# Turned exponentials read back from HBM in one transfer a tile in place of four, and the last x of a U projection split one slot sooner

## The chip, the core and the metric

The kernel runs on one core of one Trainium2 chip. The metric is device time in microseconds (us) of one execution, lower is better. The core has four engines that matter here: TensorE (PE: matmuls, and PEld: the loading of their stationary operand), VectorE (DVE), ScalarE (ACT) and GpSimd (POOL). SyncE (SP) issues most DMA transfers, ScalarE some. 16 DMA engines move the data between HBM and the on-chip memory of 128 partitions.

## What is computed

Chunked attention, then a low-rank mixer, then a two-layer network. The inputs are q, k and v of (8 batches, 8 heads, 576 positions, 64), U (576 x 32), V (32 x 576), w_ch1 (512 x 2048) and w_ch2 (2048 x 512), all float32 or wider:

```python
scores = scale * q_c @ k_c^T              # within chunks of 64 positions, per batch and head
attn = exp(scores - max(scores)); attn = attn / (sum(attn) + 1e-9)
x = attn @ v_c                            # heads side by side: (8, 576, 512)
u = x + ((x^T @ U) @ V)^T                 # mixes positions, rank 32
out = u + relu(u @ w_ch1) @ w_ch2
```

## The kernel before

**Tiles and pairs.** Two batches form a pair (four pairs, 0 to 3), and a pair has nine tiles of 128 positions (t = 0 to 8). Three tiles form a group for the two-layer network. A block is one group with one of the 16 slices of w_ch1 and w_ch2: `hidden` (line 748) makes h with 12 matmuls, ScalarE and VectorE take relu apart into a high and a low part (`relu_high`, `relu_low`, lines 756 and 761), and `project_out` (line 774) adds three times three matmuls into the output banks. So every value is carried as a high and a low float32r part, and each product is made of three.

**Two ways of ordering.** The lead (weights, tiles of pair 0, and the first blocks) is ordered by a planner with costs. From there the order is written out by hand: the loop at line 980 goes through the blocks, and each block has four slots, `j` = 0 to 3. At each slot it first runs what the dictionary `agenda` holds for that slot, in the order in which `at` put it there, and then the output products of the block before (`flush`). Slots are numbered through: `FIRST` is 128, a pair has `PAIR` = 192. Every engine does its instructions in this order, each waiting only for its own data and for the room that it writes.

**Attention of pairs 1 to 3.** ScalarE issues `permute` transfers (line 580), 288 KB each, which copy q and k in HBM into blocks of 32 (`qblocks`, `kblocks`). A `Tile` then does its steps at slots relative to its own slot s (`plan_tile`, line 901): `load` of q and k at s - 9, `turn` at s - 4 (VectorE transposes in blocks of 32), `load_v` at s + 1, `turn_ex` and `sums` at s + 2, `put_ex` at s + 3, `get_ex` at s + 6. At s itself runs `both` (line 945): the value products of the tile before (`values`, line 675), the scores of this one (line 622), its softmax up to the exponential (lines 635, 636, 642), and then `scaled` of the tile before (line 687), which makes its x. The chain of these slots is written out at line 932: tiles of pair 1 from t = 2 follow each other after 10, 10, 10, 12 and 20 slots, those with t = 7 and 8 after 11 and more.

**The turned exponentials.** The value products need the exponentials with keys on partitions. VectorE transposes within blocks of 32 (`exb`, line 653), and the blocks are moved across partitions through HBM. `put_ex` (line 657) stores 32 partitions of `exb` in each of four transfers, 512 bytes a piece, into a room of [g 4, k 32, a 4, (h i) 128]. `get_ex` (line 664) reads it back in four transfers, one for each a, to 128 partitions (g k), in pieces of 32 numbers (128 bytes) that go to `eT[:, h, a, :]`. Each of the eight is 64 KB. All are issued by SP, whose instructions wait in order: for the data, and for a semaphore to be free, of which the transfers of SP and ScalarE share eight in turn.

**U projections.** A pair has two (e = 0, 1), each over five x (`project_ops`, line 487): `high` copies x to `xh` (ScalarE, line 496), `low` makes `xl` = x - `xh` (VectorE, line 500), `product` is two matmuls on `ust` (lines 507 and 508), and the last step also evacuates y (lines 517 and 518). `plan_proj` (line 921) puts `high` of the i-th x at a slot s, `low` at s + 1 and `product` at s + 4. The five start at made - 3 to made + 1, where made is the slot at which `both` makes the last x.

**Mixes.** `plan_mix` (line 913): `low_rank` (line 535) and `add` (line 541) at s, `turn` at s + 1, `put` (line 718) of four transfers `xs<-xb` at s + 2, `get` (line 724), one transfer `uf<-xs` of 256 KB, at s + 5, and `split` (lines 737 and 738) at s + 10, which makes `uth` and `utl` for `hidden`. The first three mixes of a pair are planned from made + 8 of its fifth x on, two slots apart; the next three from made + 8 of its last.

**V in the lead.** Three transfers bring V to 128 partitions (`v_ops`, line 244): the load at line 252 and the store at line 261 with `"r (b c) -> b r c"`, b = 4, and the spread at line 265, which reads rows four times over:

```python
nc.sync.dma_start(st["all"], st["rows"].unsqueeze(0).broadcast_to([4, R, S]))
```

Most tiles that live for a short time (raw, turned and split q, k, v, `ex`, `exb`, `eT`, `xh`, `xl`, `xb`, `uf`) share one set of eight buffers of 2 KB a partition (`slot`, line 74).

## Time and profile before

| what | us |
|---|---|
| median of 3 runs | 977.58 (976.29 to 980.03) |
| the profiled execution, its own time | 977.97 |
| its span, first to last instruction | 976.2 |
| TensorE busy in the span | 927.3 (95%) |
| VectorE busy | 457.6 (47%) |
| ScalarE busy | 234.7 (24%) |
| mean granted TensorE clock | 0.982 |

A row of the profile has the engine, the line of the kernel, what is written from what, and times in us from the start of the span. PE rows overlap, since matmuls are pipelined: two rows that begin 0.24 us apart and last 0.40 us are a TensorE at work without a gap. A bracket at the end of a row tells how long the engine was idle before it and what it waited for. Rows of SPq and ACTq are instructions that issue transfers; their length is the time to issue, and the time to landing is told apart. The first 92 us are the lead, with the first attention tiles and weights; from some 236 us on the tiles go through `put_ex` and `get_ex`.

### The profile page before, as it was taken

Reading aid. Unit: us, or ns where it says so; the run is one execution under the profiler, and the core shown is the slowest. Engines: PE = TensorE matmul, PEld = TensorE weight load, DVE = VectorE, ACT = ScalarE, POOL = GpSimd, SP = SyncE. Lnnn points to the kernel's source line nnn. Section 1 sums busy time; section 2 is a strip of 40 time slices with the busy share of each in tenths; the row PEclk is TensorE's granted clock in tenths of the full one; section 3 lists DMA queues with packets and bytes.
Section 4 is the critical chain, followed back from the end, with each engine's and each line's share of the span. In section 5 each row is a group of like instructions: output and inputs, shape, how many; then the busy total and the mean of one; then the engine's idle time right before and its main releaser. Section 6 shows DMA issues by size and latency. Waiting matters only on the chain.

```text
span 976.2 us, 16189 instructions
## 1 busy us (share of the span) xinstructions
PE 927.3 (95%) x6624; PEld 819.7 (84%) x6624; DVE 457.6 (47%) x898; ACT 234.7 (24%) x413; POOL 23.7 (2%) x53
## 2 busy tenths in 40 slices
PE   5477999999999999999999999999999999999998
PEld 4355888998888888888889888898889988999997
DVE  3398998223465555543641455543551443321211
ACT  4465565111121122111221122111211122111110
POOL 7200000000000000000000000000000000000000
PEclk9778999999999999999999999999999999999999
DMA  9963237455768635542483635453241312110000
GB/s 187 200 200 114 100 132 165 65 116 129 130 124 179 139 76 122 126 113 55 105 180 56 146 67 120 110 118 77 65 117 25 90 31 65 57 42 1 33 1 33
DMA packets 298631, 97.84 MB, mean 100 GB/s; under 512 B 230140, under 2 KB 287740, under 8 KB 298556
## 3 DMA queue, kind: packets, MB, share of 16 engines
q1 hardware_dynamic: 186044, 80.28, 33.2%
q10 hardware_dynamic: 111360, 14.16, 9.2%
q0 software_dynamic: 1152, 2.36, 1.2%
q8 instruction: 52, 0.85, 0.4%
q14 instruction: 23, 0.19, 0.1%
HBM read 73.61 MB, written 37.30 MB: 114 GB/s over the span
## 4 chain that ended last, share of the span: by engine, by line
PE 85%; DVE 4%; SPq 4%; DMA 3%; issue 2%; ACT 2%; ACTq 0%; DVEq 0%
PE h L748 40%; PE o L774 38%; PE as L675 2%; PE as L622 1%; PE u L535 1%; SPq L360 1%; SPq L361 1%; DMA qblocks<-in_q_dram 1%; DMA wraw<-in_moe_w_ch_dram 1%; PE y L508 1%; SPq L297 1%; DMA eT<-exs 1%; PE y L507 1%; DVE x L786 1%; ACT hh L756 0%
## 5 line engine op out<-in xcount | busy, mean ns | idle before, releaser
L748 PE MATMUL h<-uth,w 128*128 128x384 f32 x1536 | 425.1, 339 | 3.1 <-ACT uth L737 1.4
L774 PE MATMUL o<-w,hh 128*128 128x512 f32 x1152 | 364.5, 398 | 0.0
L761 DVE SCALAR_TENSOR_TENSOR hl<-h,hh 128x384 fp32r<-128x384 f32 x192 | 106.7, 556 | 423.6 <-ACT hh L756 423.0
L748 PEld LDWEIGHTS h<-uth,w 128*128 128x128 f32 x1536 | 282.0, 188 | 12.2 <-ACT uth L737 1.9
L748 PE MATMUL h<-utl,w 128*128 128x384 f32 x768 | 260.3, 339 | 0.8 <-DVE utl L738 0.4
L774 PEld LDWEIGHTS o<-w,hh 128*128 128x128 f32 x1152 | 212.4, 188 | 36.2
L756 ACT ACTIVATE hh<-h 128x384 fp32r<-128x384 f32 x192 | 94.4, 492 | 564.2 <-PE h L748 556.5
L774 PE MATMUL o<-w,hl 128*128 128x512 f32 x576 | 227.4, 395 | 0.0
L748 PEld LDWEIGHTS h<-utl,w 128*128 128x128 f32 x768 | 144.6, 188 | 9.2 <-DVE utl L738 0.7
L774 PEld LDWEIGHTS o<-w,hl 128*128 128x128 f32 x576 | 108.4, 188 | 25.8 <-DVE hl L761 0.3
L786 DVE TENSOR_TENSOR x<-o,x 128x512 f32<-128x512 f32 x48 | 31.5, 682 | 4.8 <-PE o L774 4.7
L642 ACT ACTIVATE ex<-ex 128x512 f32<-128x512 f32 x25 | 15.8, 632 | 68.2 <-DVE ex L636 68.2
L500 DVE TENSOR_TENSOR xl<-x,xh 128x512 fp32r<-128x512 f32 x40 | 26.3, 678 | 8.8 <-ACT xh L496 8.8
L496 ACT CAST xh<-x 128x512 fp32r<-128x512 f32 x40 | 24.2, 616 | 19.6 <-DVE x L454 5.6
L635 DVE TENSOR_REDUCE mx<-as 128x4 f32<-128x256 f32 x50 | 20.9, 418 | 12.9 <-PE as L622 11.4
L541 DVE TENSOR_TENSOR x<-u,x 128x512 f32<-128x512 f32 x36 | 23.9, 677 | 4.7 <-PE u L535 4.7
L675 PEld LDWEIGHTS as<-vn,eT 64*64 64x64 f32 x800 | 15.1, 134 | 11.4 <-issue 10.4
L370 POOL DMA_DIRECT2D qkv<-in_v_dram x36 | 22.3, 635 | 4.2 <-DMA qkv<-in_v_dram 3.1
L738 DVE TENSOR_TENSOR utl<-uf,uth 128x512 fp32r<-128x512 f32 x27 | 18.4, 684 | 8.4 <-ACT uth L737 8.2
L508 PE MATMUL y<-xl,ust 128*128 128x512 f32 x40 | 17.1, 428 | 5.2 <-DVE xl L500 5.2
L636 DVE TENSOR_TENSOR ex<-as,mx 128x256 f32<-128x256 f32 x50 | 21.2, 424 | 1.7
L675 PE MATMUL as<-vn,eT 64*64 64x64 f32 x800 | 19.0, 224 | 2.9 <-DMA eT<-exs 2.3
(85 smaller groups left out, 531.8 us busy)
## 6 DMA issues: line engine op xcount, KB each, us to landing
wraw<-in_moe_w_ch_dram SPq DMA_DIRECT2D x32, 512.0 KB, 3.7
out_dram<-x SPq DMA_DIRECT2D x36, 256.0 KB, 2.0
vn<-in_v_dram SPq DMA_DIRECT2D x108, 64.0 KB, 2.6
qblocks<-in_q_dram ACTq DMA_DIRECT2D x24, 288.0 KB, 3.9
kblocks<-in_k_dram ACTq DMA_DIRECT2D x24, 288.0 KB, 4.1
xs<-xb SPq DMA_DIRECT2D x108, 64.0 KB, 1.8
uf<-xs SPq DMA_DIRECT2D x27, 256.0 KB, 2.9
exs<-exb SPq DMA_DIRECT2D x100, 64.0 KB, 1.8
```

What stands on the lines that cost most here:

```text
L370: (nc.gpsimd if early(pr, t) else nc.sync).dma_start(vn[e * C : (e + 1) * C, c, :, 0:D], v[b, e::2, s0 : s0 + C, :].rearrange("h s d -> s ...
L496: nc.scalar.copy(st["h"], x_of[pr, i + 4 * e])
L500: nc.vector.tensor_sub(st["l"], x_of[pr, i + 4 * e], st["h"])
L508: nc.tensor.matmul(ps, lhsT=lhs, rhs=st["l"], start=False, stop=(i == 4))
L541: nc.vector.tensor_add(x, st["u"], x)
L636: nc.vector.tensor_sub(self.ex[:, e].rearrange("p b h k -> p h b k"), self.sc[e].rearrange("p (h b k) -> p h b k", b=2, k=TB), mx[:, e].un ...
L675: nc.tensor.matmul(ps[e][cs, (HP + hp) * C : (HP + hp + 1) * C], lhsT=self.eT[rows, hp, 2 * c : 2 * c + 2, :].rearrange("p a i -> p (a i)" ...
L748: nc.tensor.matmul(ps[:, :GN], lhsT=w[:, z, cc], rhs=u[:, cc, :], start=(n == 0), stop=(n == 3 * NCC - 1))
L756: nc.scalar.activation(hh, ps[:, :GN], AF.Relu)
L761: nc.vector.scalar_tensor_tensor(hl, ps[:, :GN], 0.0, hh, op0=ALU.max, op1=ALU.subtract)
L774: nc.tensor.matmul(acc[j], lhsT=h[:, js], rhs=w2[f][:, z], start=(first and i == 0), stop=(final and i == 2),)
L786: nc.vector.tensor_add(x, ps, x)
```

## The change

Three edits. The room of the turned exponentials is laid out as [k 32, (g h) 16, a 4, i 32], so that what one partition (g k) of `eT` needs lies in one run of 2 KB; `get_ex` becomes one transfer, and the four of `put_ex` now write pieces of 32 numbers (128 bytes) where they wrote 128 numbers. The fifth x of a U projection has its `high`, `low` and `product` one slot sooner (`high` at made, `low` at made + 1, `product` and the evacuation of y at made + 4). The first six mixes of a pair are planned one slot sooner as a whole.

```diff
         def put_ex(self):
-            self.room = dram.tile([NQ, TB, NQ, HP * TB], F32, name="exs_" + self.n)
+            self.room = dram.tile([TB, NQ * HP, NQ, TB], F32, name="exs_" + self.n)
             for a in range(NQ):
                 nc.sync.dma_start(
-                    self.room[:, :, a].rearrange("g k x -> k g x"), self.exb[a * TB : (a + 1) * TB]
+                    self.room[:, :, a],
+                    self.exb[a * TB : (a + 1) * TB].rearrange("k g (h i) -> k (g h) i", i=TB),
                 )
 
         def get_ex(self):
             self.eT = slot(F32, "eT_" + self.n, (P, HP, NQ, TB))
-            for a in range(NQ):
-                nc.sync.dma_start(
-                    self.eT[:, :, a, :], self.room[:, :, a].rearrange("g k (h i) -> (g k) h i", i=TB)
-                )
+            nc.sync.dma_start(
+                self.eT.rearrange("p h a i -> p (h a i)"),
+                self.room.rearrange("k (g h) a i -> g k (h a i)", g=NQ),
+            )
...
         h, lo, product, *rest = projs[pr, e][i]
+        s -= i == 4
         at(s, h.run)
         at(s + 1, lo.run)
         at(s + 4, product.run, *(z.run for z in rest))
...
         for t in range(3):
-            plan_mix(pr, t, s + 7 + 2 * t)
+            plan_mix(pr, t, s + 6 + 2 * t)
...
         for t in range(3, 6):
-            plan_mix(pr, t, s + 7 + 2 * (t - 3))
+            plan_mix(pr, t, s + 6 + 2 * (t - 3))
```

## The prediction, made before the changed kernel was run

> **What bounds the kernel now.** I read the page first (these are its lines on SP's DMA queue, with packets, MB and share, and on two issues, with KB and median us to landing), then the windows and TensorE's waits from 236 us on (where the tiles with `put_ex` and `get_ex` begin), then the timeline around the tightest tiles.

> ```profile
> q1 hardware_dynamic: 186044, 80.28, 33.2%
> ...
> uf<-xs SPq DMA_DIRECT2D x27, 256.0 KB, 2.9
> exs<-exb SPq DMA_DIRECT2D x100, 64.0 KB, 1.8
> ```

> ```profile
> 236.00:976.00 740.00, 728.89 (x5040) 1.00 0.39 88
> ```

> TensorE is the bound. In the stage that the change touches it is busy 728.89 of 740.00 us, so everything that any edit can win by removing waits there is 11.1 us. The waits, in us, count and longest:

> ```profile
> PE y L508 <- DVE xl L500: 2.7, 5, 0.7
> PE as L675 <- DMA eT<-exs: 2.3, 2, 1.4
> PE h L748 <- ACT uth L737: 1.4, 1, 1.4
> PE h L748 <- DVE utl L738: 0.4, 1, 0.4
> ```

> Three sites, and the diff touches all of them: the second product of a U projection waits for `xl`, the value products wait for `eT`, and one `hidden` waits for a split.

> **The read-back.** Before, each of the four gets needs only the put with its own `a`, so puts and gets overlap. After, one get needs all four puts. I follow the last tile of this kind that has a tight follower (its values at 782.00), where no other transfer disturbs it:

> ```profile
> 774.79 1.78 SPq L660 DMA_DIRECT2D exs<-exb  x4
> 776.67 2.05 SPq L667 DMA_DIRECT2D eT<-exs  x4
> 782.00 0.69 PE L675 MATMUL as<-vn,eT 64*64 64x64 f32 x32
> ```

> The fourth put starts about 0.43 before 776.57, at 776.14, and lands 1.8 later, at 777.9. A get can start there, no later than the fourth get starts now (778.72 less 0.5). SP's queue behind it (the next tile's `vn`, `qn`, `kn` loads) is therefore held no longer than now, and nothing on TensorE pays for that wait by itself. What pays is the time the one get takes.

> What it takes: it moves 128 rows of 2 KB, as `uf<-xs` does, whose landing is 2.9. But `uf` merges (g k) into one outer step of 128; in the new room k has the larger stride, (g k) does not merge, and the source walks g = 4 on the outside. The kernel has three transfers with 4 outermost, V's load, join and spread (L252, L261, L265), and the spread is slow:

> ```profile
> L265 SPq DMA_DIRECT2D vall<-vrows x1: 549/549/549, 42.0 to 42.0; - x1
> L268 ACT CAST vst<-vall x1: 671/671/671, 49.2 to 49.2; 128x576 fp32r<-128x576 f32 x1
> ```

> Its 288 KB are used 7.2 us after the issue, though weight loads run beside it. The queue's packets say why: among q1's 186,044 the trace has 9,532 of 4 bytes, which I read as the marks that a DMA engine leaves when its share is done. 598 issues with 16 marks are 9,568; 36 are missing, which is three issues with 4 marks each. I take it that these three ran on 4 engines, and that the new get will.

> [...]

> The price of 4 engines comes from a lone `uf` transfer:

> ```profile
> 857.00:860.00 3.00, 3.00 (x17) 1.00 0.25 87
> ```

> 16 engines x 3.00 us x 0.25 = 12.0 engine-us for its 256 KB: 0.75 us on 16 engines, 3.0 on 4, so 2.25 more. Added to the lowest landing of `uf` (2.7, next fence) that is 4.95. The bounds are 2.7 (16 engines) and 7.2 (the spread). I take 4.95, and 0.8 more where a permute transfer of ACT runs beside it, which is what `eT`'s landing rises by from its lowest to its median (0 to 1.6 as bounds):

> ```profile
> L724 SPq DMA_DIRECT2D uf<-xs x27: 337/344/747, 304.6 to 865.1; - x27
> DMA to landing us min/median/max: 2.7/2.9/4.0
> ...
> L667 SPq DMA_DIRECT2D eT<-exs x100: 359/457/1222, 249.4 to 789.8; - x100
> DMA to landing us min/median/max: 2.1/2.9/3.7
> ```

> The puts change too: 512 pieces of 128 B in place of 128 of 512 B. The trace has no store to HBM in 128 B pieces from on-chip memory. Its bounds are 1.8 (now) and 2.9 (`eT`, the same pieces the other way); I take 2.0, nearer the put, because the room's address, the four issues and the bytes stay. SP's issue cost I leave at 0.43.

> Now tile by tile. For 782.00: fourth put lands 778.1, the get 783.1: stall 1.0, none now. The other tight ones:

> ```profile
> 252.69 2.15 DMA eT<-exs
> 254.98 0.75 PE L675 MATMUL as<-vn,eT 64*64 64x64 f32 x28 [1.44 <-DMA eT<-exs]
> ...
> 263.10 0.43 SPq L660
> 268.82 0.63 PE L675 MATMUL as<-vn,eT 64*64 64x64 f32 x27 [0.90 <-DMA eT<-exs]
> ...
> 276.37 2.46 SPq L667 DMA_DIRECT2D eT<-exs  x4
> 280.59 0.75 PE L675 MATMUL as<-vn,eT 64*64 64x64 f32 x28 [0.37 <-issue]
> ...
> 291.80 1.88 SPq L667 DMA_DIRECT2D eT<-exs  x3
> 298.17 0.69 PE L675 MATMUL as<-vn,eT 64*64 64x64 f32 x32
> ...
> 330.59 1.79 SPq L660 DMA_DIRECT2D exs<-exb  x4
> 337.80 0.40 PE L675 MATMUL as<-vn,eT 64*64 64x64 f32 x12
> ...
> 552.41 1.79 SPq L660 DMA_DIRECT2D exs<-exb  x4
> 559.62 1.16 PE L675 MATMUL as<-vn,eT 64*64 64x64 f32 x30
> ```

> - First tile: the fourth get starts at 252.69, when its put has landed; the new one from 252.9, landed 257.85, against 254.98 now: +2.9.
> - Second: last put issued 263.10, landed 265.1, get with a permute beside it 270.9, against 268.82: +2.1. But the first stall lowers the clock (below) and TensorE comes 1.7 later, so +0.4 remains.
> - Third: fourth get issued at 278.4 (276.37 + 2.46 less 0.43), when its put had landed; then 0.3 and 4.95: 283.65 against 280.59: +3.1.
> - 337.80: last put issued 331.95, landed 333.95, get with permute 339.7: +1.9.
> - 559.62: 553.77, 555.77, 561.5: 1.9, of which 0.5 is waited now (1.16 for a group that takes 0.69): +1.4.

> Sum with 782.00: 2.9 + 0.4 + 3.1 + 1.9 + 1.4 + 1.0 = 10.7. The tile at 298.17 has 12 slots from scores to values where these have 10 or 11: its get would start by 291.8 and land by 297.5, 0.6 ahead, and I count nothing. The rest have 15 slots or more, at least 4 us more (a block of four slots is 4.2).

> **The clock.** Rows are busy us, granted clock, DMA share, GB/s:

> ```profile
> 251.10:254.50 3.40, 2.31 (x12) 1.00 0.50 76
> 312.60:316.00 3.40, 1.58 (x7) 1.00 1.07 212
> 316.00:319.40 3.40, 3.40 (x12) 0.50 0.71 127
> ```

> A stretch of 3.4 us with 1.82 idle was followed by 3.4 us at half clock, worth 1.7; one with 1.09 idle was not. Stalls of about 4.6 (first tile) and 3.8 (third) will pay it: +3.4. Those of about 1.9 (337.80 and 559.62) may, and 1.7 each stays in the range.

> [...]

> **The last x.** In the projections of pair 1 and the second of pair 2 the last product waits:

> ```profile
> 363.35 0.40 PE L507 MATMUL y<-xh,ust 128*128 128x512 f32 x1
> 363.59 0.40 PE L508 MATMUL y<-xl,ust 128*128 128x512 f32 x1
> 364.52 0.39 PE L507 MATMUL y<-xh,ust 128*128 128x512 f32 x1
> 364.66 0.64 DVE L500 TENSOR_TENSOR xl<-x,xh 128x512 fp32r<-128x512 f32 x1
> 365.36 0.51 PE L508 MATMUL y<-xl,ust 128*128 128x512 f32 x1 [0.45 <-DVE xl L500]
> ```

> The second product starts 0.84 after the first, not 0.24, because VectorE computes `xl` behind the turn and the sums of the next tile. One slot sooner it comes ahead of both. Three such sites x 0.6 = 1.8 won. In the first projections of pairs 2 and 3 the third product waits, which the edit leaves; the last projection waits for nothing. The price is `exb` of the next tile up to 0.7 later: covered by the spare slots, except at 298, where up to 0.1 would be waited. ScalarE's extra 0.62 ahead of `hh` is covered, since `hl` is used only after the next `hidden` of 2.1.

> **The mixes one slot sooner.** The one wait of `hidden`:

> ```profile
> 309.29 3.55 DMA uf<-xs
> 314.49 0.45 PE L748 MATMUL h<-uth,w 128*128 128x384 f32 x1 [1.42 <-ACT uth L737]
> ```

> Its gets now stand behind `put_ex` on SP; one slot sooner (about 1.05) the second of them goes ahead of it and the third directly behind. Between 1.05 and all of 1.82 goes; I take all, and with it the half clock after it, 1.7: 3.5 won. The other mixes have slots to spare.

> **Sum.** +10.7 + 3.4 - 1.8 - 3.5 = +8.8. The profiled execution has a span of 976.2 and its own time is 977.97, 0.4 above the median of 977.58; the difference is the same on either. 977.6 + 8.8 = 986.4, rounded to 986.

> **Rivals.**
> 1. *The get spreads on 16 engines* (against it: the 36 marks; for it: 2 KB pieces as `uf` has). It lands 2.7 after the last put: 782.00, 337.80 and 559.62 stop waiting (-0.5), the first three move by +0.6, -0.2 and +0.8. Net +0.7 - 5.3 = -4.6: 973. It decides if the get lands in under 3.5. [...] Chance 0.20.
> 2. *Four engines, but the stalls cost no clock and the later three tiles hold*: 2.9 + 2.1 + 3.1 - 5.3 = +2.8: 980. For it: those three have no wait, or 0.5, now. Chance 0.16.
> 3. *The one slot wins nothing*: the earlier `xh` takes a buffer that a product has not freed, so `xl` and `uf` are no earlier. The losses alone are 14.1: 992. For it: ScalarE's `xh` waits for `y L507` already. Chance 0.10.

> The forecast has 0.54.

> **How the numbers follow.** 0.5% is 4.9 us, about what a measurement of this kernel can tell from no change: the limits are 972.7 and 982.5. Slower: forecast and third rival, 0.64. Rival 1 lies on the lower limit with its half us either way; I give 0.14 of it to faster (a contended put that frees earlier can only add) and 0.06 to same, which with rival 2 is 0.22. The forecast's own range is 982 (no permute beside the gets, one half clock) to 992 (1.6 for each permute and two more half clocks); the 7.2 us of the spread I leave out, since weight loads like those beside it are over in this stage. With rival 2, most of rival 3 and the upper part of rival 1 the range is 975 to 993.

> **What would show it.** Right: `eT<-exs` x25 of 256 KB with a landing near 5; q1 near 174,944 packets (38,400 more in puts, 48,000 fewer in gets, 1,500 fewer marks; 300 more marks than that if 16 engines serve it); L675 waiting for `eT` at six tiles, some 15 us in all; half clock near 258 and 284; L508's waits down to two; L748's wait for `uth` gone. Wrong: a landing under 3.5, or `hidden` still waiting near 315.

## The result, and the profile after

The changed kernel takes 1005.26 us (1004.49 to 1006.35, 4 runs), against 977.37 before in the same session: a ratio of 1.0282, 95% interval 1.0259 to 1.0305, or 28 us slower. The forecast was 986, with a range to 993. The direction was as forecast and so was the larger part of the mechanism; the loss was three times as large. In the profiled execution the span grows from 976.2 to 1004.6, by 28.4.

First the page of the changed kernel, its lines for SP's queue and the puts, and the lines of its DMA view for the transfers that stand behind the gets on SP (their landing was 4.1 and 3.5 before):

```profile
q1 hardware_dynamic: 174944, 80.27, 31.7%
...
exs<-exb SPq DMA_DIRECT2D x100, 64.0 KB, 2.2
...
qn<-qblocks SPq DMA_DIRECT2D x22, 256.0 KB, 5.3
kn<-kblocks SPq DMA_DIRECT2D x22, 256.0 KB, 5.0
```

174,944 packets is to the packet what the prediction gave for a get that leaves 4 marks. With 16 marks it would be 175,244.

Then the window from 236 us on (length, TensorE busy, clock, DMA share, GB/s) and TensorE's waits in it, in us, count and longest:

```profile
236.00:1004.00 768.00, 735.10 (x5033) 0.98 0.37 85
```

```profile
PE as L676 <- DMA eT<-exs: 16.9, 5, 6.2
PE as L676 <- issue: 7.5, 2, 4.6
PE as L622 <- DVE kT L605: 2.8, 2, 1.7
PE y L508 <- DVE xl L500: 1.3, 2, 0.7
PE h L749 <- ACT uth L738: 0.6, 1, 0.6
PE h L749 <- DVE utl L739: 0.3, 1, 0.3
```

(Behind `get_ex` the lines are one higher than before: L676 is `values`.) This is nearly the whole account. TensorE is idle for 32.9 us of this stage, not 11.1: 21.8 more. Its idle time ahead of the value products alone is 24.4 (16.9 + 7.5), not 2.7 (2.3 + 0.4). The busy time rose by 6.2 for the same matmuls, since part of them ran at half clock. 21.8 and 6.2 are 28.0 of the 28.4.

The tile that the prediction followed, now with its values at 807.27 (they were at 782.00), and its row of values on TensorE:

```profile
797.11 2.60 SPq L660 DMA_DIRECT2D exs<-exb  x4
801.34 0.55 SPq L667 DMA_DIRECT2D eT<-exs  x1
801.93 2.62 SPq L612 DMA_DIRECT2D vn<-in_v_dram  x4
...
807.27 1.14 PE L676 MATMUL as<-vn,eT 64*64 64x64 f32 x30 [2.88 <-DMA eT<-exs]
```

From the first put to the values it is now 10.16 us. TensorE is ready for them 7.2 us after the first put, as before. The four puts take 2.60 to issue, not 1.78; the get starts 2.26 after the last put's issue (799.08); and the values begin 5.93 after the get's.

Last, the clock (columns as in the window above), in windows chosen to lie on its half-rate stretches:

```profile
257.20:264.00 6.80, 5.82 (x75) 0.50 0.42 82
277.70:281.10 3.40, 3.11 (x67) 0.50 0.36 73
294.70:298.10 3.40, 3.40 (x44) 0.51 0.02 5
581.50:584.90 3.40, 3.40 (x12) 0.50 0.10 19
806.70:813.50 6.80, 6.23 (x75) 0.50 0.03 7
```

These 23.8 us at half clock stand behind five of the seven stalls of the values (6.2 us at 258.18, 4.6 at 277.99, 3.5 at 294.02, 3.2 at 580.30, 2.9 at 807.27). The kernel before had 3.4 us at half clock in this stage. The stalls of 1.2 at 313.77 and of 2.95 at 353.90 have none behind them. The trace's half-rate stretches begin at 257.20, 277.68, 294.74, 581.46 and 806.74, which are 6, 5, 84 and 66 times 3.413 us apart. In this trace and in that of the kernel before, all recorded changes of the clock within the span lie whole multiples of 3.413 us apart, to 0.002 us, so I look at what a stall takes of each stretch of 3.41 us between such times. The stretch before 806.74 and the two that share the stall of 2.95:

```profile
803.33:806.74 3.41, 1.06 (x6) 1.00 0.53 127
349.36:352.77 3.41, 1.59 (x9) 1.00 0.48 128
352.77:356.18 3.41, 2.28 (x69) 1.00 0.12 30
```

The 2.35 us idle were followed by half clock here, the 1.82 and the 1.13 were not.

### The profile page after: what moved, and what is told of

Read it like the earlier page. It is cut to its first block, busy times and chain, and to the rows that moved or that the text cites. A ratio compares the mean times of both kernels' runs of the same rounds, so it can differ in the third digit from the quotient of the medians.

```text
span 1004.6 us, 16027 instructions
## 1 busy us (share of the span) xinstructions
PE 934.3 (93%) x6624; PEld 826.6 (82%) x6624; DVE 457.5 (46%) x898; ACT 234.7 (23%) x413; POOL 23.6 (2%) x53
## 3 DMA queue, kind: packets, MB, share of 16 engines
q1 hardware_dynamic: 174944, 80.27, 31.7%
## 4 chain that ended last, share of the span: by engine, by line
PE 80%; DMA 7%; SPq 5%; DVE 4%; issue 2%; ACT 1%; DVEq 0%; ACTq 0%
PE h L749 37%; PE o L775 36%; DMA eT<-exs 3%; PE as L676 2%; PE as L622 1%; SPq L361 1%; DMA exs<-exb 1%; PE u L535 1%; SPq L360 1%; DMA qblocks<-in_q_dram 1%; PE y L508 1%; DMA xs<-xb 1%; PE y L507 1%; DMA wraw<-in_moe_w_ch_dram 1%; SPq L660 1%
## 5 line engine op out<-in xcount | busy, mean ns | idle before, releaser
L676 PEld LDWEIGHTS as<-vn,eT 64*64 64x64 f32 x800 | 16.0, 144 | 32.7 <-issue 28.5
L676 PE MATMUL as<-vn,eT 64*64 64x64 f32 x800 | 19.5, 235 | 24.4 <-DMA eT<-exs 16.9
L500 DVE TENSOR_TENSOR xl<-x,xh 128x512 fp32r<-128x512 f32 x40 | 26.1, 685 | 9.9 <-ACT xh L496 6.1
L541 DVE TENSOR_TENSOR x<-u,x 128x512 f32<-128x512 f32 x36 | 23.8, 676 | 7.3 <-PE u L535 7.3
L605 DVE STREAM_TRANSPOSE qT<-qn 128x512 f32<-128x512 f32 x25 | 17.6, 705 | 11.5 <-DMA xs<-xb 8.6
## 6 DMA issues: line engine op xcount, KB each, us to landing
out_dram<-x SPq DMA_DIRECT2D x36, 256.0 KB, 2.2
uf<-xs SPq DMA_DIRECT2D x27, 256.0 KB, 2.7
```

Of the source, the lines that this page charges most:

```text
L500: nc.vector.tensor_sub(st["l"], x_of[pr, i + 4 * e], st["h"])
L541: nc.vector.tensor_add(x, st["u"], x)
L676: nc.tensor.matmul(ps[e][cs, (HP + hp) * C : (HP + hp + 1) * C], lhsT=self.eT[rows, hp, 2 * c : 2 * c + 2, :].rearrange("p a i -> p (a i)" ...
```

## The experiments

The theory (A): the loss is the get's 4 engines, which make it land late in the tight tiles. Its rivals: (B) the loss is the chain, one get that waits for four slower puts, on any number of engines; (C) the slot moves do the harm.

### The two halves of the change apart

The first kernel has the new `put_ex` and `get_ex` and the old slots, the second the old layout and the new slots.

> The room's new layout and the one get, without the two slot moves. If the loss is all the layout's and the slots win the 5.3 us of my sum, this takes about 1010 us, and the wait of the last product for xl and of hidden for a split near 315 us are there as before. Rival: the slot moves add to the loss (exb later, VectorE held by an earlier xl); then it takes less than the changed kernel, under 1000 us.

> The two slot moves on the old layout. By my sum 5.3 us faster than before: about 972 us, with L508's waits for xl down from five to two and no half clock near 316 us. Rival (the slot moves cost): 980 us or more. A result within 2 us of before would say that the moves win at one place what they lose at another.

The layout alone takes 1008.64 us, 1.0311 of the kernel before (1.0294 to 1.0328). The slots alone take 974.68, 0.9968 (0.9957 to 0.9979): 3 us faster. So C is out, and the change is a loss of 3.1% with a gain of 0.3% on it, less than the 5.3 us expected of the slots. TensorE's waits with the slots alone:

```profile
PE as L675 <- DMA eT<-exs: 2.1, 2, 1.3
PE y L508 <- DVE xl L500: 1.3, 2, 0.7
PE h L748 <- ACT uth L737: 1.0, 1, 1.0
```

The waits for `xl` fell from five to two, as forecast; the wait for `uth` only from 1.4 to 1.0, but the 3.4 us at half clock behind it are gone.

### The number of engines

One edit on the changed kernel:

```diff
-                self.room.rearrange("k (g h) a i -> g k (h a i)", g=NQ),
+                self.room.rearrange("k (g h) a i -> (k g) (h a i)", g=NQ),
```

> The changed kernel with one edit: the get reads the room's 128 rows in the order (k g), so that they merge into one outer step of 128 (rows reach other partitions, so the output differs; the bytes, pieces and waits are the same). Theory A, the get on 4 engines is the larger part of the loss: the time from the get's issue to the values falls from 5.9 us to about 3.4 in the undisturbed tile, its stall from 3.4 to under 1, most half clocks go, and the kernel takes 978 to 988 us. Rival B, the loss is the chain (one get behind four slower puts, on any number of engines): 998 us or more.

It takes 977.77 us, 1.0005 of the kernel before (0.9993 to 1.0017), at the lower edge of what A gave. Of the 28 us, this edit takes back 27. Everything else is as in the changed kernel: the layout, the 128-byte puts, the one get behind all four. Theory B asked for 998 or more and falls. The same tile on SP and TensorE, its landing and the packets:

```profile
774.72 2.60 SPq L660 DMA_DIRECT2D exs<-exb  x4
778.96 0.33 SPq L667 DMA_DIRECT2D eT<-exs  x1
...
781.93 0.71 PE L676 MATMUL as<-vn,eT 64*64 64x64 f32 x32
```

```profile
L667 SPq DMA_DIRECT2D eT<-exs x25: 325/332/347, 251.2 to 790.5; - x25
DMA to landing us min/median/max: 2.6/2.8/4.7
```

```profile
q1 hardware_dynamic: 175244, 80.27, 32.3%
```

300 packets more, 12 marks for each of 25 gets. The get starts 4.24 after the first put, as in the changed kernel (4.23), so the chain is the same; but it lands in 2.8, and in this tile no value waits. (In the whole stage the values still wait 5.2 us, at four tiles, where the changed kernel has 24.4.) Its issue also takes 0.33, not 0.55. The trace's packets of this get and of the changed kernel's in the followed tile: first packet 0.97 after the issue against 1.32, last one ended 2.27 against 5.23. The times of the 128 packets sum to 15.9 us here and to 14.2 there, so on average 12.2 packets were under way at once here and 3.6 there, which fits 16 and 4 engines.

### Four gets again, of 32 rows each

```diff
-            nc.sync.dma_start(
-                self.eT.rearrange("p h a i -> p (h a i)"),
-                self.room.rearrange("k (g h) a i -> g k (h a i)", g=NQ),
-            )
+            for g in range(NQ):
+                nc.sync.dma_start(
+                    self.eT[g * TB : (g + 1) * TB].rearrange("p h a i -> p (h a i)"),
+                    self.room[:, g * HP : (g + 1) * HP].rearrange("k h a i -> k (h a i)"),
+                )
```

> [...] Theory A: each lands some 2.2 us after its issue; the fourth is issued 3 x 0.6 us after the first, so the values come 1.8 + 2.6 us after the first issue in place of 5.9; 985 to 993 us. Rival B: 998 us or more, since these wait for all four puts as well.

984.84 us, 1.0074 (1.0058 to 1.0090), just under the 985 to 993 that A gave. With 32 rows outermost it leaves 16 marks a transfer (q1 has 176,444 packets), and the landing of its gets is 2.1 us in the median (1.8 to 4.4). It is the same bytes in the same pieces from the same room behind the same puts as in the changed kernel, 20 us faster, so the way the rows lie in HBM is not what costs these 20 us. What it lacks to the one get on 16 engines, 7 us, goes with four issues and four landings in a row (TensorE waits 9.4 us for `eT`, ten times).

### The price of 4 engines elsewhere

The kernel before, with the mixes' room in the same order of k and g, its puts still of 512 bytes:

```diff
-            self.room = dram.tile([NQ, TB, NQ, NCC * TB], F32, name="xs_" + self.n)
+            self.room = dram.tile([TB, NQ, NQ, NCC * TB], F32, name="xs_" + self.n)
...
-                self.uf.rearrange("p a c t -> p (a c t)"), self.room.rearrange("g k a x -> (g k) (a x)")
+                self.uf.rearrange("p a c t -> p (a c t)"), self.room.rearrange("k g a x -> g k (a x)")
```

> The kernel before with the mixes' room laid out as [k, g, a, x], so that the get of uf walks g = 4 on the outside; its puts keep their 512 B pieces and the attention tiles are untouched. The price of 4 engines by itself: landing of uf from 2.9 to about 5 by my estimate, or to nearly 6 as the changed kernel's get shows; 36 x 27 / 3 = 324 packets fewer on q1. The time moves little except near 315 us, where hidden waits for uf already: plus 2 to 5 us.

990.89 us, 1.0116 (1.0097 to 1.0135), far more than the 2 to 5 us expected. q1 has 185,720 packets, 324 fewer, as expected. The place is the one named, where two of these gets follow each other (SP, then ScalarE's `split` copies, then TensorE):

```profile
311.05 1.22 SPq L722 DMA_DIRECT2D uf<-xs  x2
...
317.15 0.62 ACT L735 CAST uth<-uf 128x512 fp32r<-128x512 f32 x1 [6.35 <-DMA uf<-xs]
...
319.89 0.62 ACT L735 CAST uth<-uf 128x512 fp32r<-128x512 f32 x1 [1.74 <-DMA uf<-xs]
...
320.56 0.69 PE L746 MATMUL h<-uth,w 128*128 128x384 f32 x1 [7.95 <-ACT uth L735]
```

The first is used 6.1 us after its issue, and the second, issued 0.7 later, 2.7 after that. The trace's 256 packets of the two form one train, from 313.28 to 319.35, as if the second was served behind the first on the same engines. `hidden` waits 7.95, and the 10.2 us at half clock that go with it outlast the wait: a weight load (`PEld`) takes 0.33 us still at 325.41 and 0.19 at 326.28. When no other is beside it, a get with 4 marks has its last packet end 4.4 to 5.6 us after the issue in this run, where `uf` with 16 marks lands in 2.9 in the kernel before. Not all of the 12 us is the engine count's, though. The puts keep their 512-byte pieces, but the new room makes their issue dearer too (before, then this run):

```profile
L718 SPq DMA_DIRECT2D xs<-xb x108: 302/432/1970, 295.9 to 863.2; - x108
L718 SPq DMA_DIRECT2D xs<-xb x108: 549/598/2375, 295.4 to 877.6; - x108
```

The third get is issued 1.9 us later than in the kernel before (311.73 against 309.80), and `hidden` starts 6.1 later (320.56 against 314.49). The other 4.1 us came after the issue. So a get on 4 engines is late on another tensor as well; the run does not price the engine count by itself.

### The puts alone

The kernel before with the new puts, and four gets of 128-byte pieces, each behind its own put:

```diff
             for a in range(NQ):
                 nc.sync.dma_start(
-                    self.eT[:, :, a, :], self.room[:, :, a].rearrange("g k (h i) -> (g k) h i", i=TB)
+                    self.eT[:, :, a, :], self.room[:, :, a].rearrange("k (g h) i -> (k g) h i", g=NQ)
                 )
```

> The kernel before with the new puts alone: 128 B pieces into the new room, and four gets of 128 B pieces as before, each behind its own put and on 16 engines (they read the rows in the order (k g), so the output differs). If the puts by themselves are dear, this is where it shows: four puts take 2.6 us of SP in place of 1.8 and the last lands 2.2 after its issue in place of 1.8, so the values come about 1 us later in the three first tiles: 979 to 983 us. If only the one get behind all four makes the slower puts count: 977 to 979 us.

981.81 us, 1.0025 (1.0009 to 1.0041). The puts' issue is 0.627 each here as well, against 0.432 before (before, then this run):

```profile
L660 SPq DMA_DIRECT2D exs<-exb x100: 303/432/548, 246.7 to 787.7; - x100
L660 SPq DMA_DIRECT2D exs<-exb x100: 549/627/737, 247.0 to 789.5; - x100
```

That is a quarter of a percent, the same size as the 3 us between the slots alone (974.68) and the slots with one get on 16 engines (977.77). The time lies in the expectation's first outcome (979 to 983), so the puts cost something by themselves. On the scale of the expectation, 977.6, the ratio's interval is 978.5 to 981.6, which just touches the second. The gets of this run read rows in another order and their issue rose as well, from 0.46 to 0.58, so the puts do not carry all of it for certain.

### The clock

On the changed kernel, ahead of the values of the six tight tiles:

```diff
+            if prev and (prev.pr, prev.t) in ((1, 2), (1, 3), (1, 4), (1, 7), (2, 7), (3, 7)):
+                for _ in range(13):
+                    nc.tensor.matmul(ps[0], lhsT=w1[0][:, 0, 0], rhs=w2[0][:, 0], start=True, stop=True)
```

> The changed kernel, with 13 matmuls of 128x512 (3.0 us at full clock) whose result is thrown away ahead of the value products of the six tight tiles, where TensorE idles for 3.1 to 6.7 us. They do nothing for the output. If the half clocks after the stalls are a real part of the loss, fewer half clocks follow and the kernel is 4 to 10 us faster than the changed one, though it does 78 matmuls more: 995 to 1001 us. If the clock costs nothing by itself, it takes 1005 us or more.

999.66 us, 1.0222 (1.0192 to 1.0252), against the changed kernel's 1.0282 (1.0259 to 1.0305). TensorE works 78 matmuls of 0.23 us more, 17.7 in all, and the kernel is about 6 us faster (2 to 10 by the two intervals). Its wait for `eT` fell to

```profile
PE as L676 <- DMA eT<-exs: 7.5, 5, 2.4
```

and this stretch, which holds the first tight tile and its stall, stays at full clock (the whole stage has one stretch of 3.4 us at half clock left, from 324.98):

```profile
251.00:262.00 11.00, 8.64 (x100) 1.00 0.44 100
```

Work and remaining stall together block TensorE about as long as the stalls did, so the 6 us are, by this account, the price of the half clock in the changed kernel. It fits the 6.2 us by which its busy time had grown.

### A version that beats both

The slot moves without the layout, and the six mixes one slot sooner still (against the slots alone):

```diff
-            plan_mix(pr, t, s + 6 + 2 * t)
+            plan_mix(pr, t, s + 5 + 2 * t)
...
-            plan_mix(pr, t, s + 6 + 2 * (t - 3))
+            plan_mix(pr, t, s + 5 + 2 * (t - 3))
```

> The slot moves alone, with the six mixes one slot sooner still. What is left of hidden's wait near 314 us (1.0 and 0.3) should go: 973 to 974 us. If y is not ready a slot sooner, TensorE waits for it at low_rank, and the time is 975 us or more.

974.19 us, 0.9951 of the kernel before (0.9938 to 0.9963), the fastest here, though its interval overlaps that of the slots alone (0.9957 to 0.9979). Its waits of TensorE from 236 us on:

```profile
PE as L675 <- DMA eT<-exs: 2.2, 3, 1.2
PE y L508 <- DVE xl L500: 1.3, 2, 0.7
PE as L675 <- issue: 1.0, 1, 1.0
```

`hidden` no longer waits.

## Why the prediction was wrong in size

- **The main mechanism held.** The get leaves 4 marks (174,944 packets, exact), TensorE waits for `eT` in the tight tiles, half clocks follow, and the single edit that brings back 16 marks removes 27 of the 28 us. The runs show 4 marks a get with g = 4 outermost (the changed kernel and `uf_4_engines`), 16 with 128 rows (`one_get_16`) or 32 (`get_by_g`). That a mark stands for an engine is my reading; the 3.6 and 12.2 packets under way at once fit it.
- **The step that failed is the price of the value waits, "+10.7".** They rose by 21.7 us (24.4 from 2.7). In the chain of one tile three terms were too small. "SP's issue cost I leave at 0.43" was wrong: the fourth put of 128-byte pieces is issued 1.97 after the first, where the sum had 1.35 (+0.6). The put's 2.0 to the get's start was 2.26 (+0.3). "I take 4.95" for the get was 5.93 from issue to use (+1.0): its packets start later and spread over 3.9 us (1.32 to 5.23), where I had 3.0. Together 1.9 us: the followed tile came at 10.16 after its first put, where the sum gave 8.3.
- **The tile at 298 was not covered.** Its 0.6 us of room was smaller than these 1.9; it waits 1.2 now (its values are at 313.77), so seven tiles wait, not six.
- **In the second tile the saving did not exist.** "TensorE comes 1.7 later, so +0.4 remains" leaves out that the puts come later too. Behind the first stall `hidden` runs at half clock, VectorE waits longer for its `hl`, and `exb` stands behind it. From the softmax to the first put it is 6.63 us, where it was 4.86 (two rows before, four rows after):

```profile
256.21 0.42 DVE L635 TENSOR_REDUCE mx<-as 128x4 f32<-128x256 f32 x1 [3.29 <-PE as L622]
261.07 2.46 SPq L660 DMA_DIRECT2D exs<-exb  x4
...
260.19 0.42 DVE L635 TENSOR_REDUCE mx<-as 128x4 f32<-128x256 f32 x1 [8.36 <-PE as L622]
265.62 0.56 DVE L762 SCALAR_TENSOR_TENSOR hl<-h,hh 128x384 fp32r<-128x384 f32 x1 [3.09 <-ACT hh L757]
266.82 2.61 SPq L660 DMA_DIRECT2D exs<-exb  x4
277.99 1.14 PE L676 MATMUL as<-vn,eT 64*64 64x64 f32 x30 [4.58 <-issue]
```

So the puts lost 1.8 as TensorE did, and the tile waits 4.58, 3.7 more than before.

- **The half clock was undercounted.** Five stalls pay it, not two: 23.8 us at half rate, and some 6 us lost in place of 3.4. The prediction judged a stall by its length, with 1.82 us idle in one stretch as a sign. The same 1.82 (349.36 to 352.77) was not followed by half clock here. Where a stall fell among the stretches of 3.41 us told more here than its length: the one of 2.95 took 1.82 and 1.13 of two of them and brought no half clock, the one of 2.88 took 2.35 of one and brought 6.8 us of it.
- **"Nothing on TensorE pays for that wait by itself" missed what queues behind the get.** `qn` and `kn` land in 5.3 and 5.0 in the changed kernel, 3.7 each with the same get on 16 engines. The scores wait 2.8 us for `kT`, but along a longer path: VectorE's `qT` waits, by the profile, for a put of the mixes, and near the longer of the two waits (1.68 at 516.11) SP waited for a permute transfer of ScalarE before it went on with those puts (window 500 to 514):

```profile
DVE qT L605 <- DMA xs<-xb: 8.6, 2, 4.6
SPq L719 <- DMA qblocks<-in_q_dram: 2.4, 1, 2.4
```

That transfer was issued at 506.31, when the get issued at 500.25 had landed (506.29). With 16 engines SP waits 0.2 there and the scores 0.34. The other wait, 1.07 at 743.37, is 0.69 with 16 engines, so most of it need not be the get's.

- **Term by term**, from 236 us on: the value waits cost 21.7 us (sum: 10.7), the half clock 6.2 (sum: 3.4, less 1.7 won back near 316 us), `kT` 2.8 (sum: nothing), and the slots won 2.3 of waits (sum: 3.6). That is 28.4, against 28.0 measured and 8.8 forecast.
- **The slots won 3, not 5.3.** With the slots alone the three waits for `xl` went (1.4 us of the 1.8), and the half clock behind `hidden`; but of `hidden`'s own 1.82 only 0.5 went, because the third `uf` get stays behind `put_ex` on SP (309.65 in the kernel with the slots alone, against 309.80).
- **Rival 1 did not come true, and its number was off too.** With 16 engines my sum gave 973, and that kernel takes 977.77. The 4.8 us more are about what the new puts (2.4) and the smaller gain of the slots (2.3) add up to; no run shows the split.

What stays open: how the 1.9 us more in a tile and the queueing behind it share the stalls of the first three tiles, where permute transfers and busy semaphores differ from trace to trace. The sum of the parts is settled, not each of those three. Why a put's or get's issue costs more with the new room is open too.

## What to carry to other kernels

Before gathering transfers into one, write down the outermost step of both sides, and where it does not merge, measure that form first: here the get of 256 KB with 4 on the outside left 4 marks, not 16, its last packet ended after 5.2 us, not 2.3, and `qn` behind it landed in 5.3, not 3.7. Count the 4-byte packets of a queue: here they told the two forms apart, and the queue's total could be forecast to the packet (174,944). And where the consumer follows only 10 slots behind, price the whole chain from producer to consumer, with the issue time of each new shape as an unknown of its own; where a stall slows the consumer, ask whether it slows the producer as well.
